# Retention loads paced by three, and one more combination of the first weight in the fourth pair

## The chip, the core and the metric

One core of one Trainium2 chip runs the whole program. The metric is the device time of one execution in microseconds (us). Three runs of the kernel before gave 648.71, 649.45 and 649.96 us; the median, 649.45 us, is the time before. The engines are TensorE (PE, with its weight loads shown as PEld), VectorE (DVE), ScalarE (ACT), GpSimd (POOL) and SyncE (SP, which here only issues DMAs).

## The reference, cut to what matters

Three stages follow each other, all in fp32: retention (attention with a decay instead of a softmax), an MLP with a gated activation, and an MLP with SoLU and a layer norm.

```python
# retention: 4 batches x 8 heads, 576 positions, head size 64
scores = q @ k.T / sqrt(64);  ret = (scores * gamma_h ** (i - j) for i >= j) @ v
x = ret as [2304 tokens, 512]
h = x @ w_in            # 512 -> 2048
x = (h * sigmoid(1.702 * h)) @ w_out      # 2048 -> 512
h = x @ w2_in           # 512 -> 1024
u = h * softmax(h);  ln = (u - mean(u)) / sqrt(var(u) + 1e-6) * g_ln
out = ln @ w2_out       # 1024 -> 512
```

## The kernel before

**Retention.** The 32 heads are worked as 16 units of two heads each, and the units in 8 pairs (`for k in range(NPAIR)` in `run`). A unit's input is one tile of 128 partitions, `in`, loaded by SP in two parts: part 0 holds q and k transposed (1152 columns, 576 KB), part 1 holds k and v in their natural layout (1088 columns, 544 KB). There are six such tiles (`NU = 6`), so the load of unit u + 6 waits until everything that reads unit u has finished. `load_unit` (L255) issues one part.

In each pair `k` from the second on, TensorE works through a fixed list: `scores` of the pair (L574), `across` (L604 to L616, the product with the carried state), `states` of the next pair's first unit (L538, into the PSUM bank T), `within` of both units (L589), `states` of the next pair's second unit, and the short `last_scores` (L555). VectorE makes the state by a scan over T (`scan`, L547), masks the short scores (L564), and multiplies the scores by the decay mask (L579, four per pair). ScalarE scales v (`scale_v`, L523 and L527) and copies results out (L627); GpSimd multiplies q by the decays (`decay_q`, L511 and L513).

**Work for the next stage, slipped in.** The MLPs' weights come as 64-bit floats and are converted on VectorE (`convert`, L277 to L279). The first MLP is multiplied in a Strassen-like form with seven products, so each weight block needs four differences ("combinations") of 256 columns: `queue_combine` queues t1, t2, t3 and t4 as `sub` (L284) at a cost of 0.5 each. `slot(n)` takes queued work until n is used up. Two tuples in `run` set how much is taken in which pair: one before `across`, one before `scan`. With the tuples before, the first block's combinations are made two before the fourth pair's scan (`k` = 3), one in the fifth pair and one in the sixth.

**The DMA queue.** SP issues all loads and stores in the order of the program. Each load takes the next of eight completion semaphores in turn, and waits until the load that had the semaphore eight DMAs earlier has landed. After the units' loads stand six loads of the first weights (`load_w`), and after them the stores `xd` of the split activations (L668).

**The stage after.** `emit_h(0)` (L705) and `emit_y` (L779) begin the first MLP behind the last pair. There VectorE converts and combines the remaining weights.

Of the kernel before, what the change touches and what calls it, by code (L numbers as in the profile page):

```python
# [10 lines left out]
F32 = mybir.dt.float32  # L11
# [34 lines left out]
CQ, CK = 0, S  # L46
# [77 lines left out]
NU = 6  # L124
PLAIN = (0, 1, 2)
NPAIR = B * NP // 2
# [21 lines left out]


WARM = 7  # L150
LATE = 3
PACE = ((2, 6), (0, 6), (5, 0), (0, 6), (6, 0), (5, 0))


class Build:
# [96 lines left out]
    def const(self, name):  # L252
        lo, hi = _CC[name]
        return self.at(_M["c"] + lo, hi - lo)

    def load_unit(self, u, part):

        a, b = ((0, CKN), (CKN, CATT))[part]
        self.nc.sync.dma_start(out=self.inp[u % NU][:, a:b], in_=self.att_in[u, :, a:b])

    def load_raw(self, dst, src):

# [35 lines left out]
    def slot(self, n):  # L298
# [5 lines left out]
        for x in late:  # L304
            fn, give, spill = x
            if i >= LATE or (spill and (self.quiet or len(self.stores) > self.last)):
                self.late.append(x)
# [700 lines left out]
    def run(self):  # L1008
# [8 lines left out]
        def spin(n):  # L1017
            for _ in range(n):
                nc.tensor.matmul(wb[:, 0:P], warm, warm, start=True, stop=True)

        spin(WARM)
        self.prepare()

        def load_w():
            dst, piece = self.first_loads.pop(0)
            self.load_raw(dst, self.source(piece))

        self.load_unit(0, 0)
        self.load_consts()
        self.load_unit(0, 1)  # L1030
# [3 lines left out]
        for part in range(2):  # L1034
            self.load_unit(4, part)
        load_w()
        for part in (1, 0):
            self.load_unit(5, part)
# [3 lines left out]
        def make_x(*js):  # L1042
            for j in js:
                split_x(j)
                self.xready += 1
# [3 lines left out]
        for k in range(NPAIR):  # L1049
            u = 2 * k  # L1050
            nxt = k + 1 < NPAIR
            if k + 2 < NPAIR:
                self.decay_q(u + 4, u + 5)
            if k == 0:
                pt, o = self.bank("T0"), []
                self.scores(0)
                spin(2)
                self.scale_v(0)
                self.states(0, pt)
                o.append(self.bank("o0"))  # L1060
                self.within(0, o[0], True)
                self.scores(1)
                ends = [self.bank("e0")]
                self.last_scores(0, ends[0])
                self.last_masks(0, ends[0])
                spin(4)
                self.scale_v(1)
                self.states(1, pt)
                self.scan(0, pt)
                o.append(self.bank("o1"))  # L1070
                self.within(1, o[1], True)
                pt = self.bank("T1")
                self.scale_v(2)
                self.states(2, pt)
                ends.append(self.ybank("e1"))
                self.across(0, o, ends, False)
                self.scale_v(3)
                self.states(3, pt)
                for i in range(2):
                    self.take(i, o[i], False)  # L1080
                for i in range(2):
                    self.take(i, ends[i], True)
                self.scan(1, pt)
                self.scores(2)
                self.last_scores(1, ends[0])
                self.last_masks(1, ends[0])
                self.scores(3)
            else:
                if nxt:
                    self.scale_v(u + 2)  # L1090
                if k > 1:
                    self.scores(u)
                    self.scores(u + 1)
                o, ends = [self.bank(f"o{u}")], [self.bank(f"e{k}")]
                o.append(self.bank(f"o{u + 1}"))
                for i in ((), (), (), (), (0,), (1,), (3,), (2,))[k]:
                    sums[i]()
                self.slot((0, 0, 0, 0, 0.5, 0.5, 0, 6)[k])
                ends.append(self.ybank(f"e{u + 1}"))
                self.across(k, o, ends, True)  # L1100
                if nxt:
                    pt = self.bank(f"T{k + 1}")
                    self.states(u + 2, pt)
                for i in range(2):
                    self.take(u + i, ends[i], True)
                if not nxt:
                    steps = self.emit_h(0)
                    next(steps)
                for i in range(2):
                    self.within(u + i, o[i], False)  # L1110
                if nxt:
                    self.scale_v(u + 3)
                    self.states(u + 3, pt)
                    self.last_scores(k + 1, ends[0])
                    make_x(*((), (), (), (), (1,), (2,), (4,))[k])
                    self.slot((0, 3, 3, 1, 0, 0, 0)[k])
                    self.scan(k + 1, pt)
                    self.last_masks(k + 1, ends[0])
                for i in range(2):
                    self.take(u + i, o[i], False)  # L1120
            if k == 0:
                for i, part in ((NU, 0), (NU, 1), (NU + 1, 1)):
                    self.load_unit(i, part)
                load_w()
                self.load_unit(NU + 1, 0)
            for i in (u + NU, u + 1 + NU):
                if k and i < 2 * NPAIR:
                    for part in range(2):
                        self.load_unit(i, part)
            for _ in range((0, 0, 0, 0, 1, 1, 2, 2)[k]):  # L1130
                load_w()
            make_x(*((), (0,), (3,), (5,), (), (), (), (6,))[k])
# [202 lines left out]
```

## Time and profile before

| what | value |
|---|---|
| median of three runs | 649.45 us |
| the profiled execution's own time | 648.17 us |
| its span, first to last instruction | 646.4 us |
| PE busy | 638.0 us of the span (99%) |
| DVE, ACT, POOL busy | 448.9, 283.9, 304.5 us |
| retention (first score to first product of the MLP) | 4.4 to 62.5 us of the span |
| granted TensorE clock | 1.00 throughout |

The span is 1.8 us shorter than the profiled execution's time, and that execution is 1.28 us below the median of the runs. PE's busy time is the union of instructions whose ends are modelled, so 99% says that PE nearly always has an instruction in work, not that it could not be faster. Where a row of the timeline ends in brackets, the engine stood idle before it for that long, and the name behind the arrow is what released it; "issue" means that it waited for nothing that the profile shows.

### The profile page before, as it was taken

What the parts mean: (1) busy time and instruction counts of PE and PEld (TensorE: products, weight loads), DVE (VectorE), ACT (ScalarE), POOL (GpSimd) and SP (SyncE); (2) the same over time, 40 slices, a digit from 0 to 9 for tenths busy, and PEclk for the clock granted to TensorE, in tenths of its full rate; (3) what the DMA queues carried; (4) which work ended last, traced back from release to release, by engine and by line L of the source; (5) the groups of instructions that cost most, each with busy time, mean ns of one, the idle gap of its engine ahead of it and who ended that gap; (6) DMA issues with size and microseconds to landing.
All of it is one profiled execution on the core that took longest, in us unless ns stands there. A gap on an engine that the chain in (4) does not pass through costs nothing.

```text
span 646.4 us, 11295 instructions
## 1 busy us (share of the span) xinstructions
PE 638.0 (99%) x4316; PEld 597.9 (93%) x4316; DVE 448.9 (69%) x746; ACT 283.9 (44%) x614; POOL 304.5 (47%) x312
## 2 busy tenths in 40 slices
PE   8999999999999999999999999999999999999998
PEld 7989989999999999999999999998888888888887
DVE  2998979746477587567576454455998977787770
ACT  3566564746434343334343424343444552454231
POOL 3498595955335574336574424352324430442100
PEclk9999999999999999999999999999999999999999
DMA  8999466662575835756644959489100000000001
GB/s 330 411 416 419 179 230 242 239 234 97 188 318 203 334 131 163 275 229 256 260 149 137 361 219 337 165 301 359 48 18 32 34 17 16 34 17 16 33 32 50
DMA packets 30006, 121.78 MB, mean 188 GB/s; under 512 B 3328, under 2 KB 3840, under 8 KB 29952
## 3 DMA queue, kind: packets, MB, share of 16 engines
q1 hardware_dynamic: 29808, 120.99, 49.5%
q8 instruction: 34, 0.56, 0.3%
q14 instruction: 20, 0.16, 0.1%
q10 hardware_dynamic: 144, 0.07, 0.0%
HBM read 88.28 MB, written 32.77 MB: 187 GB/s over the span
## 4 chain that ended last, share of the span: by engine, by line
PE 83%; DVE 2%; issue 0%; ACT 0%; DVEq 0%
PE y L779 28%; PE o L933 15%; PE h L843 13%; PE h_B L705 7%; PE h_A L705 7%; PE h_C L705 7%; PE h_D L705 3%; PE zT L907 2%; DVE mem L284 1%; DVE mem L711 0%; DVE mem L653 0%; DVE conv L278 0%; DVE mem L279 0%; DVE conv L277 0%; DVE g L685 0%
## 5 line engine op out<-in xcount | busy, mean ns | idle before, releaser
L685 POOL TENSOR_TENSOR g<-mem,g 128x384 fp32r<-128x384 f32 x84 | 87.7, 1055 | 143.1 <-ACT mem L684 140.0
L293 POOL TENSOR_TENSOR win<-mem,win 128x256 fp32r<-128x256 f32 (+2 forms) x59 | 53.8, 941 | 56.7 <-ACT win L292 52.6
L779 PE MATMUL y<-g,wo 128*128 128x384 f32 x432 | 77.9, 334 | 0.0
L779 PEld LDWEIGHTS y<-g,wo 128*128 128x128 f32 x432 | 75.0, 188 | 0.3 <-DVE mem L788 0.2
L711 DVE TENSOR_TENSOR mem<-h_B,mem 128x384 f32<-128x384 f32 x48 | 26.6, 555 | 65.1 <-PE h_B L705 65.0
L788 DVE TENSOR_TENSOR mem<-y,mem 128x384 f32<-128x384 f32 x76 | 38.2, 550 | 26.6 <-PE y L779 26.4
L284 DVE TENSOR_TENSOR mem<-mem 128x256 f32<-128x256 f32 (+2 forms) x49 | 47.8, 1005 | 0.7
L662 POOL TENSOR_TENSOR x<-mem,x 128x384 fp32r<-128x384 f32 x42 | 43.4, 1065 | 5.6 <-ACT x L660 5.6
L843 PE MATMUL h<-ut,win 128*128 128x512 f32 x168 | 42.9, 390 | 0.0
L894 POOL TENSOR_TENSOR mem<-mem 128x1 f32<-128x1 f32 x18 | 10.3, 573 | 68.7 <-DVE mem L893 62.5
L293 POOL TENSOR_TENSOR ws<-mem,ws 128x512 fp32r<-128x512 f32 (+1 forms) x32 | 36.5, 1159 | 10.9 <-ACT ws L292 10.8
L933 PE MATMUL o<-u,zs 128*128 128x512 f32 (+1 forms) x171 | 41.7, 388 | 0.0
L719 ACT COPY mem<-h_A 128x384 f32<-128x384 f32 x24 | 11.6, 485 | 67.9 <-PE h_A L705 66.9
L779 PE MATMUL y<-g,wo0dt.float32r 128*128 128x384 f32 x216 | 40.8, 335 | 0.1
L779 PE MATMUL y<-g,wo1dt.float32r 128*128 128x384 f32 x216 | 40.3, 334 | 0.0
L849 DVE TENSOR_TENSOR mem<-h,mem 128x512 f32<-128x512 f32 x36 | 24.6, 687 | 22.4 <-PE h L843 12.5
L933 PE MATMUL o<-wo,zs 128*128 128x512 f32 (+1 forms) x171 | 40.0, 378 | 0.0
L779 PEld LDWEIGHTS y<-g,wo0dt.float32r 128*128 128x128 f32 x216 | 37.6, 188 | 0.6 <-DVE mem L279 0.4
L779 PEld LDWEIGHTS y<-g,wo1dt.float32r 128*128 128x128 f32 x216 | 37.7, 188 | 0.0
L843 PEld LDWEIGHTS h<-ut,win 128*128 128x128 f32 x168 | 31.4, 188 | 6.4
L933 PEld LDWEIGHTS o<-wo,zs 128*128 128x128 f32 x171 | 31.0, 188 | 6.0
L933 PEld LDWEIGHTS o<-u,zs 128*128 128x128 f32 x171 | 29.9, 189 | 5.1
(154 smaller groups left out, 1506.1 us busy)
## 6 DMA issues: line engine op xcount, KB each, us to landing
x<-xd SPq DMA_DIRECT2D x42, 768.0 KB, 8.6
xd<-x SPq DMA_DIRECT2D x21, 768.0 KB, 4.7
mem<-in_w SPq DMA_DIRECT2D x28, 512.0 KB, 5.5
in<-in_att SPq DMA_DIRECT2D x16, 576.0 KB, 9.9
in<-in_att SPq DMA_DIRECT2D x16, 544.0 KB, 9.2
out<-mem SPq DMA_DIRECT2D x17, 256.0 KB, 2.0
mem<-in_w2in SPq DMA_DIRECT2D x8, 512.0 KB, 4.0
wdt<-ws SPq DMA_DIRECT2D x8, 512.0 KB, 5.4
```

The source lines that it names most:

```text
L284: self.nc.vector.tensor_tensor(o, a, b, ALU.subtract)
L293: self.nc.gpsimd.tensor_tensor(lo, src, f32(hi), ALU.subtract)
L662: (engine or self.nc.gpsimd).tensor_tensor(x[:, 1, k], a[:, k], f32(x[:, 0, k]), ALU.subtract)
L685: engine.tensor_tensor(gs[:, 1], u, f32(gs[:, 0]), ALU.subtract)
L705: nc.tensor.matmul(o, w[:, c:c + P], x[j][:, m, k], start=(start and i == 0), stop=(stop and i == 5), skip_group_check=True,)
L711: add = lambda o, a, b: nc.vector.tensor_tensor(o, a, b, ALU.add)
L779: nc.tensor.matmul(o[m], w[:, c:c + P], gs[:, b], start=(begin and i == 0), stop=(end and i == 2),)
L788: nc.vector.tensor_tensor(y[:, m], o[m], y[:, m], ALU.add)
L843: nc.tensor.matmul(o, a[:, l, k], w[:, m], start=(start and i == 0), stop=(stop and i == 5), skip_group_check=True,)
L849: add = lambda o, a, b: nc.vector.tensor_tensor(o, a, b, ALU.add)
L907: nc.tensor.transpose(pt[:, b * P:(b + 1) * P], u[:, w:w + P], ident)
L933: nc.tensor.matmul(o[:, 0:n], z[:, a, k], w[:, b, p * n:(p + 1) * n], start=(k == 0 and i == 0), stop=(k == FB - 1 and i == 2),)
```

## The change

Two things are changed. First, a list of all loads of retention and of the first weights is kept, and from the 23rd on (`PACED = 22`, which is part 0 of unit 10) a DMA of a single element goes ahead of each load. It copies one element of the load three places back (`DEPTH = 3`) into a scratch tensor `mark` in DRAM. Reading that element makes SP wait until that earlier load has landed, and since SP issues in order, the load behind it waits as well. There are 18 such marks: 12 ahead of the loads of units 10 to 15 and 6 ahead of the loads of the first weights. Second, the two tuples change by half a unit each: `slot(0.5)` before `across` of the fifth pair becomes `slot(0)`, and `slot(1)` before the scan in the fourth pair becomes `slot(1.5)`.

```diff
+DEPTH = 3
+PACED = 22
...
+    def pace_loads(self, dst, col=0):
+
+        self.loads.append(dst[0:1, col:col + 1])
+        n = len(self.loads) - 1
+        if n >= PACED:
+            src = self.loads[n - DEPTH]
+            self.nc.sync.dma_start(out=self.mark[:, n:n + 1], in_=src)
+
     def load_unit(self, u, part):
 
         a, b = ((0, CKN), (CKN, CATT))[part]
-        self.nc.sync.dma_start(out=self.inp[u % NU][:, a:b], in_=self.att_in[u, :, a:b])
+        dst = self.inp[u % NU][:, a:b]
+        self.pace_loads(dst, 0 if part else CK)
+        self.nc.sync.dma_start(out=dst, in_=self.att_in[u, :, a:b])
...
         def load_w():
             dst, piece = self.first_loads.pop(0)
+            self.pace_loads(dst.bitcast(F32))
             self.load_raw(dst, self.source(piece))
 
+        self.loads, self.mark = [], self.dram.tile([1, 2 * 2 * NPAIR + 8], F32, name="mark")
...
-                self.slot((0, 0, 0, 0, 0.5, 0.5, 0, 6)[k])
+                self.slot((0, 0, 0, 0, 0, 0.5, 0, 6)[k])
...
-                    self.slot((0, 3, 3, 1, 0, 0, 0)[k])
+                    self.slot((0, 3, 3, 1.5, 0, 0, 0)[k])
```

On SP's queue, where unit 10 and unit 11 are asked for (tiles `in4` and `in5`), the kernel before has:

```order
L259 DMA in4_74<-in_att 128x1152
L259 DMA in4_74<-in_att 128x1088
L259 DMA in5_75<-in_att 128x1152
L259 DMA in5_75<-in_att 128x1088
L259 DMA in0_70<-in_att 128x1152
```

and the changed kernel:

```order
L264 DMA mark_151<-in2_72 1x1
L271 DMA in4_74<-in_att 128x1152
L264 DMA mark_151<-in3_73 1x1
L271 DMA in4_74<-in_att 128x1088
L264 DMA mark_151<-in3_73 1x1
L271 DMA in5_75<-in_att 128x1152
L264 DMA mark_151<-in4_74 1x1
L271 DMA in5_75<-in_att 128x1088
```

Each load keeps its place among the loads and gets one mark ahead of it; `in2` and `in3` hold units 8 and 9 there. The other engines' queues don't get a row more or less.

On VectorE, from the end of the fourth pair's masking (`s_7`) to the scan in the fifth pair, the kernel before has (T4 and T5 are the state banks that the scans of the fourth and the fifth pair read, `e3` the short scores):

```order
L579 SCALAR_TENSOR_TENSOR mem_60<-s_7_1_569,mem_60 128x512
L284 TENSOR_TENSOR mem_60<-mem_60 128x256 x2
L547 SCALAR_TENSOR_TENSOR st_77<-mem_60,T4_604 128x512
L564 TENSOR_TENSOR r2_78<-e3_581,mem_60 128x64
L564 TENSOR_TENSOR mem_60<-e3_581,mem_60 128x64
L579 SCALAR_TENSOR_TENSOR mem_60<-s_8_0_667,mem_60 128x512
L579 SCALAR_TENSOR_TENSOR mem_60<-s_8_1_668,mem_60 128x512
L579 SCALAR_TENSOR_TENSOR mem_60<-s_9_0_679,mem_60 128x512
L579 SCALAR_TENSOR_TENSOR mem_60<-s_9_1_680,mem_60 128x512
L653 TENSOR_TENSOR mem_60<-mem_60 128x768
L284 TENSOR_TENSOR mem_60<-mem_60 128x256
L547 SCALAR_TENSOR_TENSOR st_77<-mem_60,T5_717 128x512
```

and the changed kernel:

```order
L591 SCALAR_TENSOR_TENSOR mem_60<-s_7_1_574,mem_60 128x512
L296 TENSOR_TENSOR mem_60<-mem_60 128x256 x3
L559 SCALAR_TENSOR_TENSOR st_77<-mem_60,T4_609 128x512
L576 TENSOR_TENSOR r2_78<-e3_586,mem_60 128x64
L576 TENSOR_TENSOR mem_60<-e3_586,mem_60 128x64
L591 SCALAR_TENSOR_TENSOR mem_60<-s_8_0_677,mem_60 128x512
L591 SCALAR_TENSOR_TENSOR mem_60<-s_8_1_678,mem_60 128x512
L591 SCALAR_TENSOR_TENSOR mem_60<-s_9_0_689,mem_60 128x512
L591 SCALAR_TENSOR_TENSOR mem_60<-s_9_1_690,mem_60 128x512
L665 TENSOR_TENSOR mem_60<-mem_60 128x768
L559 SCALAR_TENSOR_TENSOR st_77<-mem_60,T5_726 128x512
```

One combination of 256 columns has moved from in front of the fifth pair's scan to in front of the fourth's; the rest of VectorE's list is as it was.

## Rows read from the trace of the kernel before

**Rows 1.** The page, section 1: busy us, share of the span, instructions.

```profile
PE 638.0 (99%) x4316; PEld 597.9 (93%) x4316; DVE 448.9 (69%) x746; ACT 283.9 (44%) x614; POOL 304.5 (47%) x312
```

**Rows 2.** TensorE's timeline in retention: start us, us, engine, line, operation [idle before].

```profile
20.79 0.69 PE L538 MATMUL T<-in 128*64 128x64 f32 x16
...
27.28 0.69 PE L538 MATMUL T<-in 128*64 128x64 f32 x16
...
34.36 0.69 PE L538 MATMUL T<-in 128*64 128x64 f32 x16
...
36.24 1.42 PE L589 MATMUL o<-mem,in 128*64 128x128 f32 x21 [0.55 <-issue]
...
41.64 0.45 PE L538 MATMUL T<-in 128*64 128x64 f32 x8
42.26 0.45 PE L538 MATMUL T<-in 128*64 128x64 f32 x8 [0.16 <-issue]
...
48.77 0.69 PE L538 MATMUL T<-in 128*64 128x64 f32 x16
...
51.98 2.06 PE L574 MATMUL s<-in 64*128 64x128 f32 x32
...
55.39 0.69 PE L538 MATMUL T<-in 128*64 128x64 f32 x16
...
57.65 0.63 PE L538 MATMUL T<-in 128*64 128x64 f32 x16
...
58.60 1.61 PE L574 MATMUL s<-in 64*128 64x128 f32 x24
60.40 0.71 PE L574 MATMUL s<-in 64*128 64x128 f32 x8 [0.19 <-issue]
```

**Rows 3.** The page, section 3: TensorE's instruction queue, packets, MB, share.

```profile
q8 instruction: 34, 0.56, 0.3%
```

**Rows 4.** Stretches of retention: busy us (instructions) by engine, PEclk, DMA share, GB/s.

```profile
29.93:36.24 6.31, 5.76 (x125) 5.19 (x125) 6.10 (x11) 3.69 (x10) 6.22 (x8) 1.00 1.02 417
36.24:42.26 6.02, 5.86 (x126) 5.40 (x126) 4.84 (x8) 3.82 (x11) 6.02 (x8) 1.00 1.02 417
42.26:48.27 6.01, 6.01 (x125) 5.74 (x126) 5.81 (x9) 3.70 (x9) 6.01 (x7) 1.00 1.02 414
```

**Rows 5.** The same queue's packets in 33.7:33.8 and in 45.8:45.9.

```profile
q8 instruction: 1, 0.02, 55.3%
...
q8 instruction: 1, 0.02, 58.2%
```

**Rows 6.** DMA issues in 24.74:24.76, in 43.7:43.8, in 84.1:84.2: KB, us to landing.

```profile
in<-in_att SPq DMA_DIRECT2D x1, 544.0 KB, 10.6
...
in<-in_att SPq DMA_DIRECT2D x1, 544.0 KB, 5.9
...
mem<-in_w SPq DMA_DIRECT2D x1, 512.0 KB, 3.9
```

**Rows 7.** SP's timeline: two loads of the first weights.

```profile
44.99 0.90 SPq L263 DMA_DIRECT2D win1dt.uint<-in_w  x2
```

**Rows 8.** ScalarE's timeline: scaling of unit 15's v.

```profile
55.63 0.92 ACT L523 ACTIVATE in<-in,mem 128x256 f32<-128x256 f32 x2
```

**Rows 9.** VectorE's timeline in retention.

```profile
38.17 1.22 DVE L547 TENSOR_TENSOR_SCAN st<-mem,T 128x512 f32<-128x512 f32 x1 [1.18 <-PE T L538]
...
43.55 1.23 DVE L284 TENSOR_TENSOR mem<-mem 128x256 f32<-128x256 f32 x1
44.98 1.22 DVE L547 TENSOR_TENSOR_SCAN st<-mem,T 128x512 f32<-128x512 f32 x1 [0.20 <-PE T L538]
...
58.34 1.22 DVE L547 TENSOR_TENSOR_SCAN st<-mem,T 128x512 f32<-128x512 f32 x1 [0.79 <-PE T L538]
```

**Rows 10.** The stretch from the last scan to the second step's third product (columns as rows 4).

```profile
58.34:84.10 25.76, 24.59 (x214) 22.76 (x214) 25.03 (x37) 13.74 (x31) 16.00 (x14) 1.00 0.52 216
```

**Rows 11.** TensorE's timeline in the second step of the first MLP.

```profile
84.10 1.32 PE L705 MATMUL h_B<-x,win1dt.float32r 128*128 128x384 f32 x6 [0.47 <-DVE mem L279]
```

## The prediction

> **What bounds the kernel now.** I read the page's engine totals first: PE is busy 638.0 us of the span's 646.4 [rows 1]. A change that leaves the list of matmuls alone can win only the 8.4 us that PE idles, and whatever stretches its instructions. So I went to TensorE's timeline of the stretch that the change touches, 27 to 62 us, and looked at two things: idle time before a row, and the length of a pair, from one T row (the first states of a pair) to the next. The list of matmuls is the same in each pair. The pair from 20.79 to 27.28 takes 6.49 us. The later ones take 7.08 (to 34.36), 7.28 (to 41.64), 7.13 (to 48.77) and 6.62 us (to 55.39) [rows 2]. Inside the long ones the reader finds rows with idle "issue", which no semaphore ended: 0.55 us before 36.24, 0.16 before 42.26, 0.19 before 60.40 [rows 2].
>
> What they wait for comes out of a count. TensorE's instructions come over a DMA queue of their own: 34 packets, 0.56 MB, so 16.4 KB each, and 2 x 4316 instructions over 34 packets are 254 a packet [rows 1, 3]. From 29.93 to 36.24 PE and PEld start 250 instructions, up to 42.26 another 252, up to 48.27 another 251 [rows 4]. So the idle spots lie one packet apart: at each a page of instructions ends, and the next is not there yet. I take it that a page is asked for when the one ahead of it is entered. Then the page asked for at 29.93 starts to move at 33.7 to 33.8 [rows 5], 3.8 us later, and PE goes on at 36.24, another 2.5 us later. All that while the DMA engines are full: share 1.02, 414 to 417 GB/s [rows 4]. Pages compete with the unit loads, and PE, which uses up a page in some six us, waits for them.
>
> **The change part by part.**
>
> *Marks on SP.* Eighteen DMAs of one element are added, with a wait each. In the kernel before, the load issued at 24.74 landed after 10.6 us and one at about 43.7 after 5.9 us [rows 6]. A load of 560 KB at 417 GB/s takes 1.37 us, so the first had seven loads ahead of it and the second three or four. In the changed kernel never more than three are under way. Does that still fill the engines? A round is the landing, the issue of mark and load (0.45 us each, as SP's loads lie apart [rows 7]), and at most the 3.9 us that a load took on empty queues [rows 6], of which the load's own issue is a part. That makes 0.45 + 3.9 = 4.35 us for three loads, against 3 x 1.37 = 4.1 us at full rate. So the loads keep nearly their rate. From the landing at 24.74 + 10.6 = 35.3 us, the last load of unit 15 lands four rounds later, at 35.3 + 4 x 4.35 = 52.7 us, and ScalarE takes it at 55.63 [rows 8]. Queued behind the marks on SP are the six weight loads and the stores `xd`. The last of the weights lands two rounds later, at 61.4 us; VectorE's conversions stand in its list behind the scan at 58.34 and four maskings [rows 9], so the first weight, due at 54.2 us, is there in time, and so is the sixth behind five conversions. The stores' tiles are written again only in the second step of the MLP. I cost the marks and the later issue at 0; what hides them is these 3 us of unit 15, and without that cover they cost what the second rival says.
>
> *Pages of instructions.* What the marks leave is a shorter line of loads ahead of a page. The page asked for at 29.93, when loads landed some 10 us after their issue, came after 3.8 us; the one asked for at 42.26, when a load landed after 5.9 us, came at 45.8 to 45.9, after 3.6 us [rows 5, 6]. So the wait goes down with the line, but by 0.2 us over 4.7 us of line; straight on to a line of 4.35 us it would fall by less than 0.1 us. From the other side, a whole load of 512 KB takes 3.9 us on empty queues [rows 6] and a page is a thirtieth of it, so up to some 2 us could go. The bounds are 0 and 2 us a page. I take 0.4 us: nearest to the rows of the loaded stretch, and more than their slope because a line of three runs low before each new load arrives. That is about all that a page end costs: the sums below have 0.64 us for two of them, 0.13 for one, 0.45 for one.
>
> The sum, against the clean pair of 6.49 us [rows 2]: the pair from 41.64 is 0.64 us too long, the one from 48.77 is 0.13 us, together 0.77 us up to the last pair's T. In the last pair the scores take 60.40 + 0.71 - 58.60 = 2.51 us where others take 2.06 [rows 2], 0.45 us more. The pair from 34.36 is 0.79 us too long, but its page was asked for at 29.93, when loads issued ahead of the first mark still stood in line; I take 0 of it and keep 0.79 us as a bound.
>
> *What reaches the end.* From the scan at 58.34, which waits for PE's T [rows 9], VectorE is busy 25.03 of 25.76 us [rows 10], and at the end of that stretch PE waits 0.47 us for its conversion [rows 11]. VectorE's run starts earlier by the 0.77 us. PE itself would come earlier by 1.22 us, but the 0.45 us over that only lengthen the wait at 84.10. So at most 0.77 us go through; less a tenth for page waits that shrink without going, 0.7 us. Past that point the engines wait for each other and none for a clock time, so the shift is kept.
>
> *The moved combination.* VectorE idles 1.18 us before the scan at 38.17, and a combination takes 1.23 us in the fifth pair, where the scan behind it has 0.20 us of slack [rows 9]. In the fourth pair it just about fits; in the fifth, a PE that comes more than 0.20 us earlier would otherwise find the scan late. I cost the move at 0. If the 0.55 us of idle before 36.24 went too, the scan of the fourth pair would be 0.6 us late: TensorE has 2.06 us of scores [rows 2] to do before it needs that state, which hides it; uncovered it would cost the 0.6 us.
>
> A rule bears on the pages. The Trainium skill ("Runtime: NRT & Kernel Launch", Instruction fetch mechanics) says that instruction memory is refilled in blocks of 16 KiB, 256 instructions, and that crossing a block is mostly hidden. The block agrees with the 250 to 252 instructions counted here; that crossing it is hidden does not hold in this stretch, with 0.16 to 0.55 us of idle. By the rule there is nothing to gain and the sum would be 0.
>
> Against the profiled execution the sum gives 648.17 - 0.7 = 647.5 us. That execution ran 1.28 us below the median of the runs, so on the median's footing it is 649.45 - 0.7 = 648.75, or 648.8 us.
>
> **The rivals.**
>
> *A page's wait does not depend on the line: no change, 649.4 us.* For it: between the long line and the shorter one the wait fell by just 0.2 us [rows 5, 6], the engines stay full with three loads, and the idle spot before 42.26 came when the buffers had already thinned the line. Against it: the clean pair ran with the engines as full, so a few tenths decide whether a page is late.
>
> The Trainium skill speaks for this rival ("DMA: Bandwidth & Descriptors", Queues, rings and completion order): a DMA engine goes round the queues that have work and switches at packet bounds, so a page waits for a packet of the loads and not for the line behind it. By that rule the gain is 0; the rows agree in that the wait is nearly flat, and leave open why a page needs 3.6 us to start.
>
> *The loads come late: slower.* If a round takes R us, unit 15's last load lands at 35.3 + 4R. ScalarE's scaling of it, 0.92 us [rows 8] and a short piece, about 1.2 us, must end before the T at 57.65 [rows 2], so it must land by 56.4: R = 5.28. Above that PE waits 4 (R - 5.28). At R = 5.85, 1.5 us over my sum, as if each mark cost that much on SP or the queue, that is 2.3 us: 651.7 us. For it: no row shows SP waiting behind a DMA of one element. Against it: 0.9 us of slack in each round.
>
> *More goes: faster than forecast.* If pages come 1 us sooner, the fourth pair's 0.79 us shrink too, and of the 0.47 us at 84.10 and later waits like it some 0.4 us close: 0.77 + 0.79 + 0.4 = 2.0 us, 647.5 us. For it: no page end costs as much as 1 us. Against it: the page of 36.24 is asked for before the marks bite.
>
> **How the numbers follow.** A difference of 0.2%, 1.3 us, is about what a measurement of this kernel can tell from no change. The forecast (0.2 to 1.5 us gained) gets 0.42, no change 0.24, more 0.22, late loads 0.12. Faster by over 1.3 us are nearly all of "more" (0.20) and the upper third of the forecast (0.13): 0.33. Slower by over 1.3 us are late loads (0.10) and a little of no change, where two medians differ by chance (0.03): 0.13. The rest, 0.54, is within. The likeliest case's own range is 648.0 to 649.3 us; the range for 8 in 10 reaches from 647.0 (inside "more") to 650.4 us (the mild part of late loads).
>
> **What would show it.** Right: unit loads land 4 to 5 us after their issue and the DMA share stays near 1.0; the idle "issue" at page ends past 40 us is gone and the pairs from 41.64 on take 6.5 to 6.6 us; the last pair's scan starts at 57.5 to 57.7; PE's wait near 84 us grows. Wrong: the idle spots stand as they were; or ScalarE or GpSimd wait for unit loads past 40 us; or PE is early at 62 us and no longer at 120.

## The result, and the profile after

The changed kernel takes 653.17 us (median of six runs, 652.80 to 655.77), the kernel before 649.27 us beside it (648.63 to 649.96): ratio 1.0067, 95% interval 1.0050 to 1.0084. It is slower by 3.9 us between the medians (the ratio stands for 4.4 us), outside the forecast range (647.0 to 650.4 us) and on the other side of the forecast. The rival "the loads come late" names what happened.

The profiled execution took 655.77 us, the longest of the six, and its span is 654.0 us. It holds a stretch at half clock, shown below, which costs 2.7 us; the three runs with a mean clock of 1.000 took 652.80, 653.17 and 653.47 us, so the 3.9 us of the median are not the clock's. Lines have moved by 12: L523, L538, L547, L564, L579, L604 and L705 of before are L535, L550, L559, L576, L591, L616 and L717 now.

The totals by engine, the page's section 1:

```profile
PE 641.7 (98%) x4316; PEld 600.2 (92%) x4316; DVE 449.5 (69%) x746; ACT 283.9 (43%) x614; POOL 304.3 (47%) x312
```

The span grew by 7.6 us, PE's busy time by 3.7, most of it the half clock. The rest is PE standing still. Stretches of 6 us of the kernel before (the columns of [rows 4]):

```profile
48.00:54.00 6.00, 6.00 (x132) 5.65 (x128) 5.18 (x9) 4.89 (x12) 6.00 (x7) 1.00 1.03 419
...
60.00:66.00 6.00, 5.81 (x92) 5.00 (x91) 5.93 (x9) 1.68 (x5) 2.38 (x3) 1.00 1.02 421
```

and of the kernel after:

```profile
36.00:42.00 6.00, 6.00 (x139) 5.68 (x137) 5.52 (x9) 4.11 (x11) 4.56 (x5) 1.00 0.90 300
...
48.00:54.00 6.00, 3.89 (x95) 3.45 (x92) 3.70 (x5) 2.52 (x9) 4.39 (x5) 1.00 0.85 293
...
60.00:66.00 6.00, 4.80 (x93) 4.13 (x89) 4.94 (x7) 2.13 (x5) 6.00 (x6) 1.00 0.86 287
66.00:72.00 6.00, 5.53 (x44) 4.98 (x46) 5.90 (x8) 1.47 (x4) 1.90 (x2) 0.52 0.92 310
```

Read the last two columns: from the first marks on, the data rate falls from some 420 to some 290 GB/s, while the share in which the DMA engines are busy falls only from 1.03 to 0.85 to 0.90. Between 48 and 54 us that is 17% less busy time, and 0.85 / 293 against 1.03 / 419, which is 18% more busy time per byte.

What each load takes, from the DMA issues of 33 to 56 us (KB, median us from issue to landing), before:

```profile
in<-in_att SPq DMA_DIRECT2D x4, 576.0 KB, 7.6
in<-in_att SPq DMA_DIRECT2D x4, 544.0 KB, 7.6
```

and after:

```profile
in<-in_att SPq DMA_DIRECT2D x6, 576.0 KB, 5.6
in<-in_att SPq DMA_DIRECT2D x6, 544.0 KB, 5.6
```

A load with two others under way lands 5.6 us after its issue, not the 3.9 us of a load alone [rows 6]. The round can be read on SP: a mark runs when the load three places back has landed, so of two marks with twelve loads between them the second comes four rounds after the first:

```profile
35.66 0.24 SPq L264 DMA_DIRECT2D mark<-in  x1
...
59.22 0.24 SPq L264 DMA_DIRECT2D mark<-in  x1
```

That is 23.56 us, 5.89 us a round. A mark and its load cost SP only 0.24 and 0.33 us. Unit 15's last load has landed when the mark of 59.22 runs, where the prediction had 52.7 us.

Who waits for it, first ScalarE (scaling v) and GpSimd (decaying q):

```profile
43.53 0.91 ACT L535 ACTIVATE in<-in,mem 128x256 f32<-128x256 f32 x2 [1.94 <-DMA in<-in_att]
...
52.60 0.91 ACT L535 ACTIVATE in<-in,mem 128x256 f32<-128x256 f32 x2 [3.48 <-DMA in<-in_att]
```

```profile
57.54 0.32 POOL L523 TENSOR_TENSOR in<-in,qdec 128x64 f32<-128x64 f32 x1 [1.87 <-DMA in<-in_att]
57.81 1.28 POOL L525 TENSOR_TENSOR in<-in,qdec 128x512 f32<-128x512 f32 x1
59.05 1.97 POOL L674 TENSOR_TENSOR x<-mem,x 128x384 fp32r<-128x384 f32 x2
```

then VectorE, which needs GpSimd's split of x:

```profile
61.06 2.01 DVE L296 TENSOR_TENSOR mem<-mem 128x768 f32<-128x768 f32 x1 [2.59 <-POOL x L674]
62.99 1.21 DVE L559 TENSOR_TENSOR_SCAN st<-mem,T 128x512 f32<-128x512 f32 x1
```

and at the end of both, TensorE:

```profile
33.99 0.69 PE L550 MATMUL T<-in 128*64 128x64 f32 x16
...
35.76 1.41 PE L601 MATMUL o<-mem,in 128*64 128x128 f32 x21 [0.44 <-issue]
...
41.16 0.69 PE L550 MATMUL T<-in 128*64 128x64 f32 x16
...
44.09 1.08 PE L550 MATMUL T<-in 128*64 128x64 f32 x16 [0.49 <-ACT in L535]
...
48.70 0.69 PE L550 MATMUL T<-in 128*64 128x64 f32 x16
...
53.17 1.08 PE L550 MATMUL T<-in 128*64 128x64 f32 x16 [2.04 <-ACT in L535]
...
57.77 0.93 PE L550 MATMUL T<-in 128*64 128x64 f32 x15
...
64.47 1.35 PE L616 MATMUL o<-in,st 64*64 64x128 f32 x22 [1.14 <-DVE mem L576]
...
66.47 0.38 PE L622 MATMUL e<-in,st 64*64 64x64 f32 x2 [0.53 <-DVE mem L591]
...
67.12 2.29 PE L717 MATMUL h_A<-x,win0dt.float32r 128*128 128x384 f32 x6
69.33 3.68 PE L601 MATMUL o<-mem,in 128*64 128x128 f32 x32
```

Two chains can be seen. ScalarE's late v holds up the states T twice, 0.49 and 2.04 us. GpSimd's late q holds up GpSimd's split of x, then VectorE's combination, then the scan, and PE waits 1.14 and 0.53 us at `across`. Together 4.20 us past 40 us, where before there were 0.35 us of idle "issue" [rows 2]. The MLP's first product starts at 67.12. Before, it and the next group stood here:

```profile
62.45 1.32 PE L705 MATMUL h_A<-x,win0dt.float32r 128*128 128x384 f32 x6
63.70 1.97 PE L589 MATMUL o<-mem,in 128*64 128x128 f32 x32
```

So 4.67 us are lost up to here. The two groups after it run 0.97 and 1.71 us longer in the stretch with the granted clock at 0.52, 2.68 us together. 4.67 + 2.68 = 7.35 of the span's 7.6 us; without the clock's part the execution would stand at 653.1 us, where the other five are.

### The profile page after: what moved, and what is told of

It is laid out like the page before. It is cut to its first block, busy times and chain, and to the rows that moved or that the text cites. A ratio compares the mean times of both kernels' runs of the same rounds, so it can differ in the third digit from the quotient of the medians.

```text
span 654.0 us, 11331 instructions
## 1 busy us (share of the span) xinstructions
PE 641.7 (98%) x4316; PEld 600.2 (92%) x4316; DVE 449.5 (69%) x746; ACT 283.9 (43%) x614; POOL 304.3 (47%) x312
## 4 chain that ended last, share of the span: by engine, by line
PE 82%; DVE 2%; issue 0%; ACT 0%; DVEq 0%
PE y L791 28%; PE o L945 15%; PE h L855 13%; PE h_B L717 7%; PE h_A L717 7%; PE h_C L717 7%; PE h_D L717 3%; PE zT L919 2%; DVE mem L296 1%; DVE mem L723 0%; DVE mem L665 0%; DVE conv L290 0%; DVE mem L291 0%; DVE conv L289 0%; DVE g L697 0%
```

## The experiments

Three theories were set against each other. S: with three loads under way the DMA engines starve. M: the one-element DMAs themselves hold up SP or the queue. P: TensorE's pages of instructions come late because the DMA engines are full. All kernels are the changed one with the edit shown, cut to what matters; in some of them the rows' line numbers lie one to three further.

**The slots alone.** No mark, no wait; only the combination is moved.

```diff
-PACED = 22
+PACED = 1000
```

> The two slot numbers of the change, no mark and no wait added. Theory S (the short line of loads starves the DMA engines) and theory M (each one-element DMA holds up the queue) both say that the moved combination is worth nothing either way: 649.3 us, within 0.6 of the kernel before. If the move itself were a cause, it would show here as more than 1 us.

Measured: 649.00 us (648.09 to 649.93), ratio 0.9999 (0.9990 to 1.0007). The whole loss belongs to the pacing. VectorE's third combination of the fourth pair ends before its scan, which still waits for PE:

```profile
34.95 2.59 DVE L296 TENSOR_TENSOR mem<-mem 128x256 f32<-128x256 f32 x3
38.02 1.22 DVE L559 TENSOR_TENSOR_SCAN st<-mem,T 128x512 f32<-128x512 f32 x1 [0.49 <-PE T L550]
```

**The wait without the mark, three deep.** SP waits on the landing itself; no DMA is added. The kernels wait2, wait4 and wait5 differ from this one in `DEPTH` alone.

```diff
     def pace_loads(self, ins):
-            src = self.loads[n - DEPTH]
-            self.nc.sync.dma_start(out=self.mark[:, n:n + 1], in_=src)
+            self.tc.add_manual_dep(
+                ins.ins, self.loads[n - DEPTH].ins.name,
+                mybir.DependencyInfo(mybir.DependencyClass.Sync, mybir.DependencyReason.DATA), reason="pace",
+            )
...
```

> The change with its wait for the third load in front, but the wait stands on the load itself: no one-element DMA. Theory S: still three under way, so the DMA engines still run dry; a round is shorter only by the mark's issue (about 0.4 us of 5.9), unit loads come 5 us after their issue, the traffic from 42 to 60 us stays near 300 GB/s, and the time is 651.5 to 653 us. Theory M: the traffic is back at 415 GB/s, a round is 4.1 to 4.4 us, TensorE waits for no unit load past 40 us, and the time is 648.3 to 649.5 us.

Measured: 653.06 us (651.51 to 654.01), ratio 1.0056 (1.0041 to 1.0071), as with the marks and at the upper edge of S's range. Loads land after 5.4 us and the rate is as low:

```profile
48.00:54.00 6.00, 5.93 (x134) 5.44 (x132) 5.69 (x7) 4.25 (x11) 4.18 (x5) 1.00 0.91 320
54.00:60.00 6.00, 5.12 (x111) 4.58 (x108) 3.10 (x7) 3.09 (x9) 5.07 (x7) 1.00 0.83 268
```

M falls: the loss comes without a single mark.

**The same, five deep.**

```diff
-DEPTH = 3
+DEPTH = 5
```

> As the one before, but the wait is for the fifth load in front. Theory S: five loads keep the engines full (over 400 GB/s from 42 to 60 us), no wait of TensorE for a unit load, 648.5 to 649.6 us. Theory M says the same, as there is no mark. If a page of instructions comes sooner behind five loads than behind eight, the idle issue rows past 40 us add up to less than the 0.35 us of the kernel before.

Measured: 648.50 us (647.79 to 649.50), ratio 0.9991 (0.9982 to 0.9999). The full rate is back, and past 40 us no engine waits for a unit load:

```profile
48.00:54.00 6.00, 6.00 (x128) 5.67 (x126) 5.48 (x9) 5.64 (x14) 6.00 (x7) 1.00 1.03 418
54.00:60.00 6.00, 5.78 (x132) 5.38 (x126) 5.57 (x8) 3.44 (x10) 6.00 (x5) 1.00 1.03 413
```

The page stalls are not smaller, though the loads are paced: 1.38 us past 40 us, where under 0.35 us was expected. A single profile tells little of them; without any pacing, that of slots_only has 1.16 us before 61.26. Five deep they are:

```profile
41.82 0.45 PE L551 MATMUL T<-in 128*64 128x64 f32 x8 [0.37 <-issue]
...
60.79 0.72 PE L587 MATMUL s<-in 64*128 64x128 f32 x8 [1.01 <-issue]
```

**All marks, eight deep.** The 18 one-element DMAs stay; what they wait for is eight loads back. (The eight completion semaphores are taken by marks and loads in turn, so I reckon with about four loads under way.)

```diff
-DEPTH = 3
+DEPTH = 8
```

> All 18 marks, but each reads the load eight places back, which has long landed; as marks take semaphores too, four loads are under way at most. Theory S: four nearly fill the engines, a load each 1.4 to 1.6 us, 649 to 650.5 us. Theory M: the marks still hold up the queue, a load each 1.9 to 2.0 us as in the changed kernel, and 652 us or more.

Measured: 648.74 us (647.97 to 650.31), ratio 0.9996 (0.9987 to 1.0005), under the 649 to 650.5 us that S had. Marks cost nothing that can be measured. Loads land after 6.7 (576 KB) and 5.5 us (544 KB) at 370 GB/s, like those of four deep below. TensorE's pairs bear on theory P: the two from 41.35 on are clean at 6.42 and 6.43 us, with the DMA engines at a share of 1.02 and 0.95, and behind them a stall of 0.59 us stands:

```profile
42.00:48.00 6.00, 6.00 (x137) 5.68 (x134) 4.77 (x9) 3.79 (x11) 5.42 (x7) 1.00 1.02 409
48.00:54.00 6.00, 6.00 (x140) 5.74 (x139) 5.79 (x9) 5.84 (x14) 6.00 (x7) 1.00 0.95 322
```

```profile
41.35 0.69 PE L550 MATMUL T<-in 128*64 128x64 f32 x16
...
47.77 0.69 PE L550 MATMUL T<-in 128*64 128x64 f32 x16
...
54.20 0.69 PE L550 MATMUL T<-in 128*64 128x64 f32 x16
...
59.60 0.71 PE L586 MATMUL s<-in 64*128 64x128 f32 x8 [0.59 <-issue]
```

**Four deep, without marks.**

```diff
-DEPTH = 3
+DEPTH = 4
```

> Pacing without marks, four loads under way. Theory S, by bytes: with three under way a load took 5.4 us from issue to landing, so to keep 415 GB/s 2.2 MB have to be under way; four loads are 2.3 MB, just enough: over 400 GB/s from 42 to 60 us, no wait for unit loads, 648.5 to 649.5 us. The rival, that a fixed toll per round stays however many are under way, has the traffic near 340 GB/s and 650 us or more.

Measured: 649.26 us (648.09 to 650.13), ratio 1.0001 (0.9992 to 1.0010). The time is that of before, but the rate is not; the expectation of over 400 GB/s missed:

```profile
48.00:54.00 6.00, 6.00 (x140) 5.68 (x137) 6.00 (x9) 5.05 (x12) 5.10 (x6) 1.00 0.98 386
54.00:60.00 6.00, 6.00 (x136) 5.62 (x128) 4.17 (x5) 2.88 (x9) 6.00 (x6) 1.00 0.95 311
```

The expectation of no wait for unit loads missed too: GpSimd waits 0.90 us for a q before 53.75, and PE 0.67 and 0.53 us behind VectorE before 60.68 and 62.69. ScalarE's chain has room: in the kernel before, unit 15's last load, issued at 44.57, lands 7.8 us later, some 3 us before ScalarE takes it at 55.63 [rows 8]. Why PE's 1.20 us don't show in the median stays open.

**Two deep, without marks.**

```diff
-DEPTH = 3
+DEPTH = 2
```

> As the three-deep wait without marks, but two loads under way. If the data rate follows from how much is under way (a load with one other under way lands some 5 us after its issue, by the 3.9 us of a lone load and the 5.4 us with two others): 1.12 MB in 5 us, about 220 GB/s past 40 us and 2.5 us per load; ScalarE's and GpSimd's waits for loads grow by about 0.6 us for each of the last nine unit loads, 4 to 6 us in all: median 656 to 660 us. If instead the three-deep loss was a fixed delay of each hand-over on SP's queue (0.6 us per load, whatever the depth), the rate stays near 290 GB/s and the median near 653 us.

Measured: 659.29 us (658.14 to 661.02), ratio 1.0161 (1.0144 to 1.0179): the loss goes on growing, as S has it, though part of it is the lower clock shown at the end. By the expectation's rival the rate would have stayed near 290 GB/s and the time near 653 us. From 33 to 56 us the rate is 239 GB/s, the loads land after 4.5 (576 KB) and 5.1 us (544 KB).

Put together, over the same 33 to 56 us, one profile a row (the last run below is the second of five deep):

| loads under way | us from issue to landing (576, 544 KB) | GB/s | ratio to before |
|---|---|---|---|
| 2 | 4.5, 5.1 | 239 | 1.0161 |
| 3 | 5.4, 5.4 | 300 | 1.0056 |
| 4 | 6.7, 6.3 | 368 | 1.0001 |
| 5 | 6.8, 7.2 | 416 | 0.9991 |
| 5, second run | 7.0, 6.9 | 391 | 0.9991 |
| before | 7.6, 7.6 | 415 | 1 |

**Only the weights paced.** The six loads of the first weights wait three deep, without marks as in the run before; the units' loads don't wait.

```diff
-PACED = 22
+PACED = 34
```

> Three under way only for the six loads of the first weights; the unit loads are free as in the kernel before. Theory S with slack: the weights land some 4 us later, nobody waits for them before 63 us, and the time is that of the kernel before within 0.8 us: 648.5 to 649.8 us. If the later weights or the stores behind them cost the changed kernel part of its 3.9 us, this is 650.5 us or more.

Measured: 648.54 us (647.91 to 649.42), ratio 0.9993 (0.9984 to 1.0002). The rate falls to 321 and 294 GB/s between 48 and 60 us and costs nothing there: the weights had slack, the units' loads had not enough.

**Half the bytes.** No pacing (`PACED = 1000`); the units from 10 on load half the columns of each part.

```diff
+        if u >= 10:
+            b = a + (b - a) // 2
+            dst = self.inp[u % NU][:, a:b]
```

> Nothing paced; of units 10 to 15 only the first half of each part's columns is loaded, so the result of these units is not the reference's. It halves the traffic from about 37 to 45 us. Theory P (pages of instructions are late because of the full DMA engines): the idle issue rows past 40 us shrink to under 0.2 us in all, the pairs take 6.5 to 6.6 us, and the time is 647.6 to 648.6 us. Rival: pages are late whatever the traffic, the idle rows stay, 649.0 to 649.8 us.

Measured: 648.81 us (648.30 to 649.56), ratio 0.9998 (0.9989 to 1.0007). With the engines no longer full, the stalls between 38 and 60 us are gone, and the one left stands where the rate is back at 415 to 421 GB/s:

```profile
42.00:48.00 6.00, 6.00 (x136) 5.68 (x136) 6.00 (x9) 3.75 (x10) 6.00 (x7) 1.00 0.62 188
48.00:54.00 6.00, 6.00 (x142) 5.80 (x144) 5.73 (x9) 4.53 (x12) 6.00 (x7) 1.00 0.84 306
```

```profile
42.57 0.69 PE L553 MATMUL T<-in 128*64 128x64 f32 x16
...
49.05 0.69 PE L553 MATMUL T<-in 128*64 128x64 f32 x16
...
55.47 0.87 PE L553 MATMUL T<-in 128*64 128x64 f32 x15
...
60.72 0.71 PE L589 MATMUL s<-in 64*128 64x128 f32 x8 [0.18 <-issue]
```

The pairs take 6.48 and 6.42 us, the clean pair 6.49 [rows 2]. That is what P expects, but it doesn't single P out: marks8 has pairs as short with all the bytes. Halving the bytes also shortens the line (loads land after 3.8 and 3.9 us), so traffic and line aren't told apart. The worth is not shown either: the time lies between P's 647.6 to 648.6 us and the rival's 649.0 to 649.8 us, the ratio is 0.1 us below 1, and the interval holds 0 as well as 0.7 us.

**The changed kernel without the last two decays.** GpSimd leaves out `decay_q` of units 14 and 15, so it doesn't wait for their q.

```diff
-            if k + 2 < NPAIR:
+            if k + 3 < NPAIR:
```

> The changed kernel, but GpSimd leaves out the decays of q for the last pair (units 14 and 15), whose result is then not the reference's. If the last pair's late scan comes from GpSimd's waiting for these units' loads (decays, then the split of x, then VectorE's combination, then the scan), the two waits of the last pair, 1.7 us, go: 651.2 to 652.0 us. If TensorE's waits for scaled v are all that counts, the time stays at 652.8 to 653.5 us.

Measured: 651.19 us (649.20 to 652.21), ratio 1.0027 (1.0016 to 1.0039), at the lower edge of the expected 651.2 to 652.0 us. About half of the loss is gone. The rate is nearly as low as with the decays, 293 to 309 GB/s from 42 to 60 us, but of the waits of 1.14 and 0.53 us behind VectorE 0.16 us are left (the profiled execution took 649.34 us, the second shortest of nine, so its waits may be small ones):

```profile
58.26 1.08 PE L550 MATMUL T<-in 128*64 128x64 f32 x16 [0.31 <-ACT in L535]
...
62.96 0.34 PE L622 MATMUL e<-in,st 64*64 64x64 f32 x2 [0.16 <-DVE mem L591]
```

So GpSimd's chain carries about 2 of the 3.9 us: 1.7 by the medians, 2.6 by the ratios. That is at most what the late loads cost on it, for the edit also takes the decays' own work, twice 0.32 and 1.28 us, off GpSimd's list. The rest is put down to ScalarE's chain because of the waits before T; no run takes that chain out.

**Five deep again.** The same kernel, to see if its first interval held.

> A second measurement of the five-deep wait, whose first one (ratio 0.9991, 0.9982 to 0.9999) stood at the edge. If its 0.6 us were real, the median is again 0.4 to 0.8 us under the kernel before with an interval below 1; if it was chance, the ratio is 0.9995 to 1.0005 with 1 inside the interval.

Measured: 648.37 us (647.86 to 649.61), ratio 0.9991 (0.9982 to 1.0000). Twice 0.9991: a gain of about 0.6 us is suggested, not shown, as the intervals end at 0.9999 and 1.0000. Moving the combination alone gave 0.9999, so it would come from the pacing. It isn't the stalls that shrink: this run's profile has 0.45 us of idle "issue" before 37.42 and 0.60 before 61.25. Where the 0.6 us would come from stays open. The rate of the first profile isn't kept in this one: 363 to 369 GB/s from 42 to 60 us, at a share of 0.98 to 1.00.

## Why the prediction was wrong, point by point

**The marks on SP: the step that failed.** The prediction took "at most the 3.9 us that a load took on empty queues" as the landing of a load that has two others under way. That was the time of a load that shares nothing, a floor where it was used as a ceiling. Measured were 5.4 us without and 5.6 us with marks, and the round was 5.89 us where 4.35 stood. The claim that "the loads keep nearly their rate" fell with it, 290 for 417 GB/s. The prediction had its own threshold, R = 5.28 us, and the true round lay beyond it. By its formula 4 (5.89 - 5.28) = 2.4 us, 651.9 us on the sum's footing without the gain in pages (649.45 + 2.4). The sum had the marks and the later issue at 0; they cost 3.9 us.

**What the rival lacked.** It was right in its mechanism and short in size: 2.3 us at its round of 5.85 us, where 3.9 us were lost. It followed v to ScalarE and T and left out the other reader of a unit, q to GpSimd. GpSimd's list is in order, so the split of x waited behind the late decays, VectorE's combination behind the split, and the scan behind the combination. The run without the last decays puts up to some 2 us on this chain. What spoke against the rival, 0.9 us of slack in each round, was counted from the 4.35 us that failed. And its example laid the longer round on the marks, which cost nothing that can be measured (marks8); what made it longer is the landing of 5.4 us that stands without any mark (wait3).

**Pages of instructions.** The stalls at page ends are there in most runs; that a shorter line of loads cures them is not shown, and what makes a page late stays open. Five deep the line was hardly shorter (the landing went from 7.6 to 7.0 us, the share stayed at 1.02 to 1.03), and stalls of 0.37 and 1.01 us remained. In marks8 two pairs were clean at a share of 1.02 and 0.95. With three weights under way (weights3) a stall of 0.48 us stood before 60.78, at a share of 0.92 and 294 GB/s from 54 to 60 us. With half the bytes none stood between 38 and 60 us. In the changed kernel the two stalls past 40 us are gone, but PE had waited 2.04 us for data ahead of the second. Neither the line nor full engines alone sort these.

The Trainium skill ("DMA: Bandwidth & Descriptors", Queues, rings and completion order) says that a DMA engine takes turns between the queues that have work, packet by packet. The stall of weights3 behind a short line agrees with that; the clean pairs of marks8 don't speak for it, and no run shows the turns themselves.

The stall before 35.76 stayed (0.44 us), as the prediction had it, since it placed the asking for that page ahead of the marks. The gain of 0.7 us came in no run: where the pairs were clean, in marks8 and with half the bytes, the ratios are 0.9996 and 0.9998, each with 1 in its interval.

**The moved combination.** Right: 2.59 us of combinations fit. The scan behind them still waits for PE, 0.49 us with the slots alone and 0.48 us in the changed kernel. In four other profiles (wait3, wait4, wait5_again, half_loads) it doesn't wait, but PE doesn't wait for the state there either.

**What reaches the end.** Right in kind: the shift is kept. The product that stood at 84.10 [rows 11] starts at 91.48 after a wait of 0.48 us, 7.4 us later, against 7.6 us at the end. In all twelve profiles, from 562.2 to 562.5 us lie between the start of this product and the end. The sign of the shift was the other one.

**What would have shown it.** "Wrong: ScalarE or GpSimd wait for unit loads past 40 us" is what the trace has, with up to 3.48 us (ScalarE) and 1.87 us (GpSimd) for one load.

## What to carry to other kernels

A pacing wait sets how many bytes are under way, and that sets the rate: measure a load's landing with the same number of others under way, not alone, before dividing by it. Here 2.9 MB under way (five loads) moved 416 and 391 GB/s in two profiles, and 1.7 MB (three) 300 GB/s, with marks 291. When a transfer becomes late, follow every reader of its tile down every engine's queue; the second reader's chain carried up to about half of the loss.

## What the runs showed that was not expected

A load's landing grows by only some 0.5 to 1.1 us with each further load under way (4.8, 5.4, 6.5, 7.0 us for two to five, the mean of the two sizes), less than the 1.37 us that its bytes take at the full rate; only at five does the rate come up to that of before, in one of two profiles. The 18% more busy time per byte is not tied to few loads alone: slots_only, where nothing is paced, moves 349 GB/s at a share of 1.01 from 54 to 60 us, about as much more per byte. Its cause stays open, and so does how much of the lower rate is due to it.

TensorE's granted clock fell to its lower level (1.2 of 2.4 GHz) behind the new idle times: 0.52 from 66 to 72 us in the changed kernel, after waits of 1.14 and 0.53 us in a stretch where PE was busy 4.80 of 6 us; and in the two-deep kernel, after a stretch with 4.08 of 6 us:

```profile
42.00:48.00 6.00, 4.08 (x74) 3.42 (x74) 1.15 (x2) 2.74 (x9) 3.45 (x4) 1.00 0.78 237
48.00:54.00 6.00, 6.00 (x102) 5.75 (x104) 4.88 (x9) 2.25 (x7) 2.73 (x4) 0.72 0.81 248
```

It isn't bound to happen: after the longer wait of 2.04 us in the changed kernel, in a stretch with PE busy 3.89 of 6 us, the clock stayed at 1.00 from 54 to 60 us, and three of the six runs of the changed kernel have a mean clock of 1.000. Where the clock fell, a wait on data cost a second time, 2.7 us in the profiled execution.
